# Linear attention and a gated long convolution on one core: two moves in GpSimd's early order, and one add-and-subtract product of batch 6 given to GpSimd

## The chip, the core and the metric

The kernel runs on one core of a Trainium2 chip. A core has a matrix engine (TensorE, PE in the profile), a vector engine (VectorE, DVE), a scalar engine (ScalarE, ACT), a general engine (GpSimd, POOL) and an engine that only issues transfers (SyncE, SP). Each runs its own instructions strictly in program order, and waits on semaphores for the others. Sixteen DMA engines move data between the memory HBM and the on-chip buffer SBUF; transfers are put to them through queues, here mainly SP's and POOL's. TensorE writes its results to eight banks of PSUM, which POOL cannot read.

The metric is the device time of one execution, in microseconds (us). The kernel before took a median of 304.77 us over three runs, from 303.0 to 306.35.

## The reference

There are 8 batches, 8 heads, 576 positions, and 64 channels a head (512 in all). A linear attention is followed by a long convolution with gates:

```
phi(x) = concat(exp(p), exp(-p)),  p = x @ w_phi - max|x @ w_phi|
kv  = phi(k)^T v;   z = sum over positions of phi(k)
att = (phi(q) kv) / (phi(q) z + 1e-6)
x1, x2, x3 = att @ w_proj   (three parts of 512)
y   = x1 * irfft(rfft(x2) * rfft(filter)) * x3
out = y @ w_out
```

The two Fourier transforms over 576 positions are done as matrix products with tables of cosines.

## The kernel before

The program is a list of words, PLAN (lines 31 to 200). Each word names a method, its arguments and often a PSUM bank: `f2,DVE,6,0,0` calls `f2` on VectorE for batch 6, half 0, part 0; `Pk,2,0@6` works in bank 6. `run` (line 1056) goes through the words in order and emits the instructions of each. So the order of the words is the order on each engine's queue, written out by hand, and the engines run apart from one another as far as the data allow. Work of neighbouring batches is interleaved: while batch b is in its convolution, batch b+1 is in its attention.

A batch goes through these stages. Its q, k and v are loaded by POOL's queue (`load`, line 598, 576 KB each, cast to 16 bits on the way). q and k are transposed by a DMA transpose on SP's queue (`trh`, line 627, two of each a batch), only for batch 0 partly by TensorE (`pt`). TensorE makes the projections (`Pk`, `Pq`, `Qn`), DVE the maxima over features (`maxk`, `maxq`, line 732), ACT the exponentials (`ex`, line 718). The maxima of q go through ACT (`mhi`), POOL (`mlo`, line 756, tile mh) and a small TensorE transpose (`trm`, line 760) with its copy (`trme`, tile mT) before `Pq` can subtract them. v is multiplied with the factors of k (`em` by ACT, `vs`, line 774, by POOL or DVE: tiles vp and vm). `KV` (line 789) sums over positions: in each half-head it runs 18 matmuls with vp, then 18 with vm. `NE` (line 803) makes the attention's numerator and denominator, `rc` and `xn` (lines 817, 822) divide.

Then comes the convolution. `f1` (line 871) and `f2` (line 877) are two levels of adds and subtracts (a butterfly) on the attention's output xn, through SD to xf, each on a half of the batch (two of four column blocks); they make the transform shorter. `F` (line 880) is the forward transform: for each block two matmuls with the table Dt (line 883) and four with D on xf (line 887). `X1`, `X2`, `X3` project (lines 944 and 922), `Y1` multiplies with the filter's spectrum (line 932), `m3` adds (line 936), `I` (line 997) transforms back, `ym` gates, `O` (line 1044) is the last product, `st` stores.

The filter's own spectrum is made once, early. Eight pieces of 128 KB are loaded into fl (`fl_load`, line 483) and the middle rows into flt (`fl_loadt`, line 489), all on SP's queue. `fa` (line 498, twice, on POOL) makes sums and differences of the rows, the tile fs; these are the row sums. `zl` (lines 531 to 536, ten small copies on POOL) lays out the lowest frequencies' columns of the cosine tables, the tiles zl2 and zlt. `ft` (on ACT) casts flt to f5 (f in the profile). `Hd` (lines 541 to 551, on TensorE) multiplies: `Hd,4` needs zl2, zlt, fs and f5, and comes first; the others need fs and f5. `He` scales the result into the tables HTe, HTo and H5 that `Y1` reads.

POOL's queue around the first part of the change, in order: `vs,POOL,m,0,0`, `load,k,2`, `vs,POOL,p,0,1`, `w_load,proj,0`, `w_load,proj,1` (the first two of three 512 KB parts of w_proj, line 588), `zl`, `fa,1`, `fa,0`, `f1,POOL,0,0,0`, `load,v,1`, `mlo,1`, `load,q,2`. On SP's queue the transposes `trh,k,2,0` and `trh,k,2,1`, which read what `load,k,2` brings, stand behind `trx,0,1` (line 841, a transpose of xn) and ahead of `trh,q,2,0`.

Around the second part, POOL runs `vs,POOL,p,7,0`, `vs,POOL,m,7,0`, `vs,POOL,p,7,1`; DVE runs `X1e,6,3` and then `f2,DVE,6,0,0` and `tmt,6`. TensorE's order is `F,6,1`, `F,6,0`, `Pq,7,1`, `KV,7,0`. Both blocks of `F` named here belong to half 0, and need the `f2` of that half.

Of the kernel before, what the change touches and what calls it, by code (L numbers as in the profile page):

```python
# [179 lines left out]
KV,7,1@6 m3,POOL,6,0 rc,7,1@4 Y1,6,4@3 xn,7,1@4 Pqt,7@0 KVe,ACT,7,1@6 NE,7,0@2 trx,7,1 exqt,p,7@0  # L180
Pq,7,2@6 rc,7,0@2 exqt,m,7@0 xn,7,0@2 NE,7,3@4 ex,q,p,7,2@6 X2,6,3@0 trx,7,0 f1,POOL,7,0,1
rc,7,3@4 xn,7,3@4 ex,q,m,7,2@6 X2,6,2@3 Y1,6,3@0 f1,POOL,7,0,0 st,SP,5,0,0 X1,6,2@1 st,SP,5,2,0
Y1,6,2@3 f2,POOL,7,0,0 NE,7,2@4 X1e,ACT,6,2@1 X3,6,2@7 m3,DVE,6,1 NEt,7@1 rc,7,2@4 xn,7,2@4
X3,6,3@0 trx,7,2 f1,DVE,7,1,1 I,6,2@4 rct,7@1 f1,POOL,7,1,0 xnt,7,1@1 xnt,7,0@1 X3,6,0@3 Ie,6,2@4
trx,7,3 tm,6,2@7 f2,POOL,7,0,1 Ip,6,2@4 I,6,1@1 Im,6,2@4 trxt,7 tm,6,0@3 I,6,3@6 f2,POOL,7,1,1
Ie,6,1@1 Im,6,1@1 Ie,6,3@6 Ip,6,1@1 X3,6,1@1 f2,POOL,7,1,0 Ip,6,3@6 F,7,1@4 Im,6,3@6 tm,6,1@1
F,7,0@2 ym,POOL,6,2 Fe,ACT,7,1@4 F,7,2@6 Fe,ACT,7,0@2 F,7,3@4 Fe,DVE,7,2@6 ym,POOL,6,1 X1,7,1@1
tm,6,3@0 X1,7,2@7 Fe,DVE,7,3@4 ym,POOL,6,3 I,6,0@2 X2,7,2@5 Ie,6,0@2 X1e,ACT,7,2@7 X2,7,0@4
X1e,ACT,7,1@1 Y1,7,2@5 Xl,ACT,7 X2,7,1@6 Im,6,0@2 X1,7,0@7 Ip,6,0@2 Y1,7,0@4 ym,POOL,6,0 X2,7,3@1
Y1,7,1@6 X1t,7@3 X2,7,4@2 Y1,7,3@1 m3,POOL,7,0 X3,7,2@4 X1te,DVE,7@3 O,6,3@0 Y1,7,4@2 O,6,1@5  # L190
m3,POOL,7,1 Oe,ACT,6,3@0 X1e,ACT,7,0@7 st,SP,6,3,1 X3t,7@0 Oe,ACT,6,1@5 X1,7,3@2 st,SP,5,3,1
tmt,7@0 tm,7,2@4 st,SP,5,3,0 I,7,2@6 st,SP,6,3,0 X3,7,0@5 Ie,7,2@6 st,SP,6,1,0 X1e,ACT,7,3@2
Im,7,2@6 st,SP,6,1,1 I,7,1@0 Ip,7,2@6 tm,7,0@5 ym,POOL,7,2 I,7,0@6 Ie,7,1@0 Ip,7,1@0 I,7,3@4
Ie,7,0@6 Ip,7,0@6 X3,7,1@3 Ie,7,3@4 Im,7,1@0 Im,7,0@6 O,6,0@2 tm,7,1@3 ym,POOL,7,0 X3,7,3@0
Ip,7,3@4 Oe,ACT,6,0@2 Im,7,3@4 ym,POOL,7,1 st,SP,6,0,1 O,6,2@2 tm,7,3@0 st,SP,6,0,0 ym,DVE,7,3
Oe,ACT,6,2@2 O,7,0@1 st,SP,6,2,0 yt,DVE,7 O,7,1@7 Oe,ACT,7,0@1 st,SP,6,2,1 st,ACT,7,0,1 O,7,4@5
st,SP,7,0,0 Oe,ACT,7,1@7 O,7,2@6 st,SP,7,1,1 st,ACT,7,1,0 Oe,DVE,7,4@5 O,7,3@0 st,SP,7,4,1
# [912 lines left out]
```

## Time and profile before

| what | value |
|---|---|
| time, median of three runs | 304.77 us (303.0 to 306.35) |
| the profiled execution's own time | 301.6 us |
| its span in the trace | 299.8 us |
| mean granted clock of TensorE | 0.983 of full speed |
| read from HBM, written | 33.75 MB, 9.44 MB |

The profile is of one execution, and its start times count from the start of the span. A row of a timeline has the start and the duration in us, the engine, the line of the code, the operation, the output and input tiles, how many instructions are merged, and in square brackets the time for which the engine stood idle before it with what ended that idle time. Durations of neighbouring rows on one engine overlap a little, so what a row takes of its engine's time is the distance to the next start. A stretch in the table of busy times gives from:to, its length, and then busy time and count of instructions for PE, PE's weight loads, DVE, ACT and POOL, the granted clock, the share of the DMA engines' time, and GB/s. A row of DMA issues ends with the size and the median time from issue to landing.

### The profile page before, as it was taken

To read this page: it belongs to the slowest core of one execution; us is meant where nothing else is said; L and a number is where in the kernel's file an instruction comes from. 1 tells how busy PE (TensorE), PEld (TensorE's weight loads), DVE (VectorE), ACT (ScalarE), POOL (GpSimd) and SP (SyncE) were. 2 spreads that over 40 slices of the span, in tenths; PEclk is the share of its full clock that TensorE was granted. 3 is DMA by queue.
4 is the path that set the end of the run, shared out by engine and by line. 5 is a ranking of instruction groups with operands and counts; after the bars stand their busy time and mean duration, and the time that the engine had idled before them with its cause. 6 is when DMAs were issued, how large, how long until landed. Compare 5 with 4: busy or idle time off the path is not lost.

```text
span 299.8 us, 10196 instructions
## 1 busy us (share of the span) xinstructions
PE 278.9 (93%) x4303; PEld 198.9 (66%) x4303; DVE 261.8 (87%) x450; ACT 218.2 (73%) x353; POOL 220.5 (74%) x185
## 2 busy tenths in 40 slices
PE   8848679999999999999999999999999898999992
PEld 3525546688677786777776776776687575876761
DVE  8999978899989997889889999899987998897762
ACT  2899988984789777868898498877568978623330
POOL 8008788699888888988979895767686984775640
PEclk9986999999999999999999999999999999999997
DMA  7999999899989979996999626767621641320336
GB/s 112 190 203 181 212 160 198 108 201 180 120 124 190 140 133 183 181 240 124 163 212 198 113 43 148 113 132 135 103 50 29 134 97 37 72 47 0 73 86 195
DMA packets 72734, 40.18 MB, mean 134 GB/s; under 512 B 53040, under 2 KB 67504, under 8 KB 72688
## 3 DMA queue, kind: packets, MB, share of 16 engines
q1 hardware_dynamic: 57472, 22.62, 42.8%
q0 software_dynamic: 14816, 16.25, 34.6%
q8 instruction: 33, 0.54, 0.7%
q10 hardware_dynamic: 400, 0.66, 0.7%
q14 instruction: 13, 0.11, 0.1%
HBM read 33.75 MB, written 9.44 MB: 144 GB/s over the span
## 4 chain that ended last, share of the span: by engine, by line
PE 71%; DVE 10%; DMA 5%; SPq 4%; ACT 3%; issue 2%; POOL 2%; DVEq 0%; ACTq 0%; POOLq 0%
PE ps L944 16%; PE ps L922 11%; PE ps L1044 10%; PE ps L997 7%; PE ps L789 4%; PE ps L803 4%; SPq L627 3%; DMA qn<-in_q_dram 3%; PE ps L883 3%; PE ps L887 3%; DMA flt<-in_moe_filter_fft_dram 2%; PE ps L690 2%; PE ps L953 2%; PE ps L656 2%; PE ps L696 2%
## 5 line engine op out<-in xcount | busy, mean ns | idle before, releaser
L944 PE MATMUL ps<-xT,wproj 128*128 128x256 bf16 x512 | 64.2, 273 | 0.0
L944 PEld LDWEIGHTS <-wproj 128*128 128x128 bf16 x512 | 48.3, 98 | 10.3
L1033 POOL TENSOR_TENSOR yT<-cv,x1s 128x576 bf16<-128x576 f32 x30 | 38.8, 1302 | 16.2 <-DVE cv L1018 13.1
L732 DVE TENSOR_REDUCE mq<-ps 128x8 f32<-128x1024 f32 (+1 forms) x40 | 44.1, 1112 | 3.8 <-PE ps L663 2.4
L732 DVE TENSOR_REDUCE mk<-ps 128x8 f32<-128x1024 f32 (+1 forms) x40 | 44.4, 1113 | 1.0 <-PE ps L671 0.3
L774 POOL TENSOR_TENSOR vp<-vn,vp 128x1152 bf16<-128x1152 bf16 x15 | 33.0, 2201 | 11.0 <-ACT vp L768 10.6
L877 POOL TENSOR_TENSOR xf<-SD 128x512 bf16<-128x512 bf16 x27 | 31.3, 1170 | 8.4 <-PE ps L922 4.4
L936 POOL TENSOR_TENSOR T<-T,T 128x1024 bf16<-128x1024 bf16 x15 | 31.8, 2124 | 6.0 <-DVE T L932 6.0
L1044 PE MATMUL ps<-wout,yT 128*128 128x512 bf16 x144 | 35.6, 379 | 0.2
L718 ACT ACTIVATE Ekm<-ps 128x1024 bf16<-128x1024 f32 x32 | 33.1, 1039 | 2.9 <-PE ps L656 2.3
L718 ACT ACTIVATE Eqm<-ps 128x1024 bf16<-128x1024 f32 x32 | 33.0, 1030 | 2.4 <-PE ps L696 2.2
L718 ACT ACTIVATE Eqp<-ps 128x1024 bf16<-128x1024 f32 x32 | 32.5, 1028 | 2.7 <-PE ps L696 2.5
L718 ACT ACTIVATE Ekp<-ps 128x1024 bf16<-128x1024 f32 x32 | 32.9, 1036 | 1.7 <-DVE mk L732 1.1
L774 POOL TENSOR_TENSOR vm<-vn,vm 128x1152 bf16<-128x1152 bf16 x13 | 28.6, 2204 | 4.3 <-ACT vm L768 4.3
L922 PE MATMUL ps<-wproj,XF 128*128 128x512 bf16 x128 | 31.0, 380 | 0.0
L871 POOL TENSOR_TENSOR SD<-xn 128x512 bf16<-128x512 bf16 x23 | 26.3, 1161 | 5.7 <-DVE xn L822 5.7
L997 PE MATMUL ps<-inv,T 128*128 128x288 bf16 x192 | 27.8, 286 | 0.7 <-DVE xnt L834 0.6
L1018 DVE TENSOR_TENSOR cv<-es,ps 128x288 f32<-128x288 f32 x64 | 25.8, 444 | 1.6 <-ACT es L1015 1.4
L301 ACT COPY o<-ps 128x512 f32<-128x512 f32 x25 | 14.7, 598 | 15.2 <-PE ps L1044 15.1
L1015 ACT COPY es<-ps 128x288 f32<-128x288 f32 x32 | 12.7, 402 | 16.9 <-PE ps L997 15.0
L985 DVE TENSOR_TENSOR x1s<-ps,x1s 128x512 bf16<-128x512 f32 x32 | 21.9, 685 | 2.7 <-PE ps L944 2.2
L822 DVE TENSOR_TENSOR xn<-ps,r 128x512 bf16<-128x512 f32 x32 | 21.8, 687 | 0.9
(175 smaller groups left out, 657.8 us busy)
## 6 DMA issues: line engine op xcount, KB each, us to landing
out_dram<-o SPq DMA_DIRECT2D x67, 128.0 KB, 2.9
vn<-in_v_dram POOLq DMA_DIRECT2D x8, 576.0 KB, 8.0
qn<-in_q_dram POOLq DMA_DIRECT2D x7, 576.0 KB, 8.8
kn<-in_k_dram POOLq DMA_DIRECT2D x7, 576.0 KB, 8.9
wproj<-in_moe_w_proj_dram POOLq DMA_DIRECT2D x3, 512.0 KB, 9.6
fl<-in_moe_filter_fft_dram SPq DMA_DIRECT2D x8, 128.0 KB, 2.9
out_dram<-o ACTq DMA_DIRECT2D x5, 128.0 KB, 3.2
qn<-in_q_dram POOLq DMA_DIRECT2D x2, 288.0 KB, 5.2
```

What stands on the lines that cost most here:

```text
L718: self.nc.scalar.activation(e, p, AF.Exp, bias=0.0, scale=1.0 if g == "p" else -1.0)
L732: self.nc.vector.tensor_reduce(out=out, in_=src, axis=AX.X, op=ALU.max, apply_absolute_value=True)
L774: self.eng(eng).tensor_tensor(out=t[:, :, :, 0:64], in0=self.at("vn", b)[:, 2 * X:2 * X + 2], in1=t[:, :, :, 64:65].to_broadcast([128, 2, ...
L871: self.eng(eng).tensor_tensor(out=o[:, :, 2 * i:2 * i + 2, :], in0=x[:, :, 0:2, :], in1=x[:, :, 2:4, :], op=ALU.subtract if i else ALU.add)
L877: self.eng(eng).tensor_tensor(out=o[:, :, 2 * i:2 * i + 2, :], in0=x[:, :, 0:4:2, :], in1=x[:, :, 1:4:2, :], op=ALU.subtract if i else ALU ...
L922: self.mm(self.pb(0), l, w[:, kt, 512:1024], start=(kt == 0), stop=(kt == 3))
L936: self.eng(eng).tensor_tensor(out=Y, in0=Y, in1=self.at(f"T{2 * e + 1}", b), op=ALU.add)
L944: self.mm(o[:, d], w[:, kt, f0 + 128 * m:f0 + 128 * m + 128], y[:, 1, ::-1, ::-1] if d else y[:, 0], start=(kt == 0), stop=(kt == 3))
L997: self.mm(self.pb(e, 0, 288), l, inv[:, 2 * e + i if i < 2 else 4 + e, :], start=(i == 0), stop=(i == 2))
L1018: self.nc.vector.tensor_tensor(out=self.turn_of("cv", (b, m))[:, :, odd, :], in0=self.turn_of("es", (b, m)).rearrange("p (x t) -> p x t", ...
L1033: self.eng(eng).tensor_tensor(out=self.at("yT", b)[:, m, 0:SEQ], in0=self.turn_of("cv", (b, m)).rearrange("p x h t -> p (x h t)"), in1=sel ...
L1044: self.mm(self.pb(0), y[:, kt, 128 * c:128 * c + 128], w[:, kt, :], start=(kt == 0), stop=(kt == 3))
```

## The change

Three words of PLAN are moved; the total of 1509 words and every method stay.

1. `load,k,2` moves seven places on: on POOL's queue it now stands behind `vs,POOL,p,0,1` and `w_load,proj,0`, ahead of `w_load,proj,1`.
2. `zl,POOL` moves from ahead of `fa,POOL,1` to behind `fa,POOL,0`, just ahead of `f1,POOL,0,0,0`.
3. `f2,DVE,6,0,0` becomes `f2,POOL,6,0,0`, and stands two places later in the list; on POOL's queue that is between `vs,POOL,p,7,0` and `vs,POOL,m,7,0`.

```
-vs,DVE,p,0,0 load,k,2 fl_loadt ex,q,m,0,1@4 Pk,1,1@0 maxq,1,3@2 KV,0,0@6 vs,POOL,p,0,1
-w_load,proj,0 ex,q,p,0,1@4 maxk,1,1@0 KVe,ACT,0,0@6 Pqt,0@4 Qnt,1@2 exqt,p,0@4 NE,0,1@6 maxqt,1@2
-w_load,proj,1 exqt,m,0@4 rc,0,1@6 ex,k,m,1,1@0 NE,0,0@2 xn,0,1@6 zl,POOL fa,POOL,1 Pq,0,3@4
-rc,0,0@2 trx,0,1 ex,k,p,1,1@0 xn,0,0@2 Qn,1,2@6 maxq,1,2@6 ptx,0,0@2 ex,q,p,0,3@4 Qn,1,1@0
-ex,q,m,0,3@4 cols_h ptxe,DVE,0,0@2 maxq,1,1@0 trh,k,2,0 Pq,0,2@2 fa,POOL,0 f1,POOL,0,0,0 ft,ACT
+vs,DVE,p,0,0 fl_loadt ex,q,m,0,1@4 Pk,1,1@0 maxq,1,3@2 KV,0,0@6 vs,POOL,p,0,1 w_load,proj,0
+load,k,2 ex,q,p,0,1@4 maxk,1,1@0 KVe,ACT,0,0@6 Pqt,0@4 Qnt,1@2 exqt,p,0@4 NE,0,1@6 maxqt,1@2
+w_load,proj,1 exqt,m,0@4 rc,0,1@6 ex,k,m,1,1@0 NE,0,0@2 xn,0,1@6 fa,POOL,1 Pq,0,3@4 rc,0,0@2
+trx,0,1 ex,k,p,1,1@0 xn,0,0@2 Qn,1,2@6 maxq,1,2@6 ptx,0,0@2 ex,q,p,0,3@4 Qn,1,1@0 ex,q,m,0,3@4
+cols_h ptxe,DVE,0,0@2 maxq,1,1@0 trh,k,2,0 Pq,0,2@2 fa,POOL,0 zl,POOL f1,POOL,0,0,0 ft,ACT
...
-X1e,ACT,6,0@0 X3t,6@2 Fe,DVE,6,2@6 F,6,3@4 X1e,DVE,6,3@1 O,5,2@0 Fe,ACT,6,3@4 f2,DVE,6,0,0 trm,7@3
-vs,POOL,m,7,0 X1t,6@1 Oe,ACT,5,2@0 F,6,1@4 X1te,ACT,6@1 st,SP,5,2,1 trme,ACT,7@3 F,6,0@6 tmt,6@2
+X1e,ACT,6,0@0 X3t,6@2 Fe,DVE,6,2@6 F,6,3@4 X1e,DVE,6,3@1 O,5,2@0 Fe,ACT,6,3@4 trm,7@3
+f2,POOL,6,0,0 vs,POOL,m,7,0 X1t,6@1 Oe,ACT,5,2@0 F,6,1@4 X1te,ACT,6@1 st,SP,5,2,1 trme,ACT,7@3
...
```

The lines left out at the end hold the same words in the same order, only broken at other places.

More of the change, by code (lines that the diff above doesn't have):

```diff
@@ L174 @@
 st,SP,5,4,0 f2,POOL,6,1,0 X1e,DVE,6,1@7 X1,6,0@0 Oe,ACT,5,3@2 maxk,7,2@3 vs,POOL,p,7,0 F,6,2@6
-X1e,ACT,6,0@0 X3t,6@2 Fe,DVE,6,2@6 F,6,3@4 X1e,DVE,6,3@1 O,5,2@0 Fe,ACT,6,3@4 f2,DVE,6,0,0 trm,7@3
-vs,POOL,m,7,0 X1t,6@1 Oe,ACT,5,2@0 F,6,1@4 X1te,ACT,6@1 st,SP,5,2,1 trme,ACT,7@3 F,6,0@6 tmt,6@2
-Fe,ACT,6,1@4 st,SP,5,0,1 Pq,7,1@0 em,m,7,1 Fe,DVE,6,0@6 KV,7,0@3 ex,q,m,7,1@0 Xl,DVE,6
-vs,DVE,m,7,1 em,p,7,1 Pq,7,0@5 ex,q,p,7,1@0 X2,6,1@7 KVe,DVE,7,0@3 vs,POOL,p,7,1 ex,q,m,7,0@5
-Pq,7,3@1 Y1,6,1@7 ex,q,p,7,0@5 X2,6,0@0 X2,6,4@3 ex,q,p,7,3@1 Y1,6,0@0 NE,7,1@4 ex,q,m,7,3@1
@@ L180 @@
[L180 to L197, printed above, removed]
+X1e,ACT,6,0@0 X3t,6@2 Fe,DVE,6,2@6 F,6,3@4 X1e,DVE,6,3@1 O,5,2@0 Fe,ACT,6,3@4 trm,7@3
@@ new lines @@
+f2,POOL,6,0,0 vs,POOL,m,7,0 X1t,6@1 Oe,ACT,5,2@0 F,6,1@4 X1te,ACT,6@1 st,SP,5,2,1 trme,ACT,7@3
+F,6,0@6 tmt,6@2 Fe,ACT,6,1@4 st,SP,5,0,1 Pq,7,1@0 em,m,7,1 Fe,DVE,6,0@6 KV,7,0@3 ex,q,m,7,1@0
+Xl,DVE,6 vs,DVE,m,7,1 em,p,7,1 Pq,7,0@5 ex,q,p,7,1@0 X2,6,1@7 KVe,DVE,7,0@3 vs,POOL,p,7,1
+ex,q,m,7,0@5 Pq,7,3@1 Y1,6,1@7 ex,q,p,7,0@5 X2,6,0@0 X2,6,4@3 ex,q,p,7,3@1 Y1,6,0@0 NE,7,1@4
+ex,q,m,7,3@1 KV,7,1@6 m3,POOL,6,0 rc,7,1@4 Y1,6,4@3 xn,7,1@4 Pqt,7@0 KVe,ACT,7,1@6 NE,7,0@2
+trx,7,1 exqt,p,7@0 Pq,7,2@6 rc,7,0@2 exqt,m,7@0 xn,7,0@2 NE,7,3@4 ex,q,p,7,2@6 X2,6,3@0 trx,7,0
@@ new lines @@
+f1,POOL,7,0,1 rc,7,3@4 xn,7,3@4 ex,q,m,7,2@6 X2,6,2@3 Y1,6,3@0 f1,POOL,7,0,0 st,SP,5,0,0 X1,6,2@1
+st,SP,5,2,0 Y1,6,2@3 f2,POOL,7,0,0 NE,7,2@4 X1e,ACT,6,2@1 X3,6,2@7 m3,DVE,6,1 NEt,7@1 rc,7,2@4
+xn,7,2@4 X3,6,3@0 trx,7,2 f1,DVE,7,1,1 I,6,2@4 rct,7@1 f1,POOL,7,1,0 xnt,7,1@1 xnt,7,0@1 X3,6,0@3
+Ie,6,2@4 trx,7,3 tm,6,2@7 f2,POOL,7,0,1 Ip,6,2@4 I,6,1@1 Im,6,2@4 trxt,7 tm,6,0@3 I,6,3@6
+f2,POOL,7,1,1 Ie,6,1@1 Im,6,1@1 Ie,6,3@6 Ip,6,1@1 X3,6,1@1 f2,POOL,7,1,0 Ip,6,3@6 F,7,1@4 Im,6,3@6
+tm,6,1@1 F,7,0@2 ym,POOL,6,2 Fe,ACT,7,1@4 F,7,2@6 Fe,ACT,7,0@2 F,7,3@4 Fe,DVE,7,2@6 ym,POOL,6,1
@@ new lines @@
+X1,7,1@1 tm,6,3@0 X1,7,2@7 Fe,DVE,7,3@4 ym,POOL,6,3 I,6,0@2 X2,7,2@5 Ie,6,0@2 X1e,ACT,7,2@7
+X2,7,0@4 X1e,ACT,7,1@1 Y1,7,2@5 Xl,ACT,7 X2,7,1@6 Im,6,0@2 X1,7,0@7 Ip,6,0@2 Y1,7,0@4 ym,POOL,6,0
+X2,7,3@1 Y1,7,1@6 X1t,7@3 X2,7,4@2 Y1,7,3@1 m3,POOL,7,0 X3,7,2@4 X1te,DVE,7@3 O,6,3@0 Y1,7,4@2
+O,6,1@5 m3,POOL,7,1 Oe,ACT,6,3@0 X1e,ACT,7,0@7 st,SP,6,3,1 X3t,7@0 Oe,ACT,6,1@5 X1,7,3@2
+st,SP,5,3,1 tmt,7@0 tm,7,2@4 st,SP,5,3,0 I,7,2@6 st,SP,6,3,0 X3,7,0@5 Ie,7,2@6 st,SP,6,1,0
+X1e,ACT,7,3@2 Im,7,2@6 st,SP,6,1,1 I,7,1@0 Ip,7,2@6 tm,7,0@5 ym,POOL,7,2 I,7,0@6 Ie,7,1@0 Ip,7,1@0
@@ L198 @@
+I,7,3@4 Ie,7,0@6 Ip,7,0@6 X3,7,1@3 Ie,7,3@4 Im,7,1@0 Im,7,0@6 O,6,0@2 tm,7,1@3 ym,POOL,7,0
+X3,7,3@0 Ip,7,3@4 Oe,ACT,6,0@2 Im,7,3@4 ym,POOL,7,1 st,SP,6,0,1 O,6,2@2 tm,7,3@0 st,SP,6,0,0
+ym,DVE,7,3 Oe,ACT,6,2@2 O,7,0@1 st,SP,6,2,0 yt,DVE,7 O,7,1@7 Oe,ACT,7,0@1 st,SP,6,2,1 st,ACT,7,0,1
+O,7,4@5 st,SP,7,0,0 Oe,ACT,7,1@7 O,7,2@6 st,SP,7,1,1 st,ACT,7,1,0 Oe,DVE,7,4@5 O,7,3@0 st,SP,7,4,1
 st,ACT,7,4,0 Oe,DVE,7,2@6 st,SP,7,2,1 st,ACT,7,2,0 Oe,DVE,7,3@0 st,SP,7,3,0 st,ACT,7,3,1
```

## The prediction

> **What bounds the kernel now.** First the page's busy times, its chain that ended last, and the busy times by stretch.
>
> ```profile
> PE 278.9 (93%) x4303; PEld 198.9 (66%) x4303; DVE 261.8 (87%) x450; ACT 218.2 (73%) x353; POOL 220.5 (74%) x185
> ...
> PE 71%; DVE 10%; DMA 5%; SPq 4%; ACT 3%; issue 2%; POOL 2%; DVEq 0%; ACTq 0%; POOLq 0%
> ...
> 50.00:240.00 190.00, 187.73 (x3090) 137.18 (x3087) 170.74 (x269) 150.85 (x243) 158.46 (x117) 1.00 0.85 140
> 246.00:260.00 14.00, 13.02 (x299) 9.13 (x298) 11.60 (x17) 11.44 (x18) 8.16 (x6) 1.00 0.16 35
> ```
>
> PE is busy for 187.73 of the 190 us from 50 to 240 (the third number of a stretch), so an earlier start of that stretch shifts the rest with it. The change works ahead of it, at 26 to 42 us, and behind it at 246, where PE is idle 0.98 of 14 us. In both places I follow the chain of waits: which engine stands, and for whom.
>
> At 26 to 42 us the timelines of POOL, then ACT, then PE, show (start, duration, in brackets the idle time before and its releaser):
>
> ```profile
> 26.49 0.81 POOL L598 DMA_DIRECT2D kn<-in_k_dram  x1
> 27.31 2.46 POOL L774 TENSOR_TENSOR vp<-vn,vp 128x1152 bf16<-128x1152 bf16 x1
> 29.73 1.54 POOL L588 DMA_DIRECT2D wproj<-in_moe_w_proj_dram  x2
> 31.26 0.23 POOL L531 COPY zl<-D 128x32 bf16<-128x32 bf16 x1
> ...
> 32.62 0.23 POOL L536 COPY zlt<-Dt 64x64 bf16<-64x64 bf16 x1
> 34.97 4.66 POOL L498 TENSOR_TENSOR fs<-fl 128x1024 bf16<-128x1024 f32 x2 [2.12 <-DMA fl<-in_moe_filter_fft_dram]
> 39.60 1.15 POOL L871 TENSOR_TENSOR SD<-xn 128x512 bf16<-128x512 bf16 x1
> 40.70 0.78 POOL L598 DMA_DIRECT2D vn<-in_v_dram  x1
> 41.49 0.26 POOL L756 TENSOR_TENSOR mh<-mq,mh 128x36 bf16<-128x36 f32 x1
> ...
> 35.30 0.62 ACT L301 CAST f<-flt 64x512 bf16<-64x512 f32 x1 [0.62 <-DMA flt<-in_moe_filter_fft_dram]
> ...
> 40.48 1.02 ACT L718 ACTIVATE Ekp<-ps 128x1024 bf16<-128x1024 f32 x1
> 42.08 0.27 ACT L301 COPY mT<-ps 128x128 bf16<-128x128 bf16 x1 [0.58 <-PE ps L760]
> ...
> 39.61 0.37 PE L541 MATMUL ps<-f,zlt 64*128 64x512 bf16 x1 [0.64 <-ACT Ekp L718]
> ...
> 41.81 0.23 PE L760 MATMUL ps<-ident,mh 128*128 128x128 bf16 x1 [0.63 <-POOL mh L756]
> ```
>
> The filter's landing holds two engines: POOL stands 2.12 us before the row sums (fs, word fa), ACT 0.62 before the cast of flt (word ft). From there ACT's exponentials run to 41.50 and PE's first filter matmul waits for one of them. POOL's mh (mlo,1) comes late behind the sums, and PE's transpose trm,1 waits 0.63 for it; ACT then 0.58 for trm.
>
> **Step 1: the load of k of batch 2 moves behind vp and the first weights.** The same four instructions stand on POOL from 26.49 to 31.26, in another order: vp 26.49 to 28.91 (27.31 to 29.73 took 2.42), first weights 0.77, k 0.82, second weights 0.77, done at 31.27. Nothing is won in POOL's time; k is issued 3.2 us later (29.7), the first weights 0.8 earlier (28.9). What changes is the traffic beside the filter's loads on SP's queue. SP's issues, then times to landing by issue:
>
> ```profile
> 23.05 2.23 SPq L483 DMA_DIRECT2D fl<-in_moe_filter_fft_dram  x4
> ...
> 26.99 1.05 SPq L483 DMA_DIRECT2D fl<-in_moe_filter_fft_dram  x2
> 28.09 0.49 SPq L489 DMA_DIRECT2D flt<-in_moe_filter_fft_dram  x1
> 31.71 1.23 SPq L841 DMA_TRANSPOSE xT<-xn  x1
> 36.34 6.07 SPq L627 DMA_TRANSPOSE kT<-kn  x2
> ...
> fl<-in_moe_filter_fft_dram SPq DMA_DIRECT2D x2, 128.0 KB, 2.9
> ...
> fl<-in_moe_filter_fft_dram SPq DMA_DIRECT2D x1, 128.0 KB, 5.2
> ...
> fl<-in_moe_filter_fft_dram SPq DMA_DIRECT2D x1, 128.0 KB, 7.1
> flt<-in_moe_filter_fft_dram SPq DMA_DIRECT2D x1, 128.0 KB, 7.2
> ...
> kn<-in_k_dram POOLq DMA_DIRECT2D x1, 576.0 KB, 9.7
> ...
> xT<-xn SPq DMA_TRANSPOSE x1, 10.7
> ```
>
> Issued around 24.4, before k, a piece of 128 KB lands after 2.9 us; issued at 26.99, 27.61 and 28.09, behind k's issue, after 5.2, 7.1 and 7.2. With k away until 29.7, between ends of 2.9 and 7.2, I take 2.9, the row for the same transfer with POOL's queue quiet: the last fl at 27.61 + 2.9 = 30.5, flt at 31.0. The other end is 34.7 and 35.3, as now.
>
> What k's lateness costs: now it lands at 26.49 + 9.7 = 36.2 and SP issues its transposes at 36.34. Behind the first weights I bound it by the 3.2 us later issue: 39.4. SP waits there; behind it stand only transposes for batch 2 (q, from 51 us) and xTt. The first reader of kT comes at 58.55:
>
> ```profile
> 58.55 0.39 PE L656 MATMUL ps<-wphi,kT 64*128 64x128 bf16 x8
> ...
> 45.89 1.92 PE L944 MATMUL ps<-xT,wproj 128*128 128x256 bf16 x16
> ...
> 50.95 2.14 POOL L774 TENSOR_TENSOR vm<-vn,vm 128x1152 bf16<-128x1152 bf16 x1
> ...
> 54.77 0.42 PE L789 MATMUL ps<-vm,Ekm 64*128 64x65 bf16 x16
> ```
>
> The two transposes are issued by 42.4 now and so by 45.6; even 10 us to land leave 3. The xT transpose landed at 42.4 (31.71 + 10.7) for a reader at 45.89; with less queued ahead of it on SP it comes no later. Cost nothing, cover 3 us in each case.
>
> **Step 2: zl moves behind the row sums.** Its ten copies (31.26 to 32.85, 1.59 us) lay inside the wait for the filter. Now fa starts when POOL is free and the filter is there: 31.3. Sums 4.63 (34.97 to 39.60): 35.9. zl 1.59: 37.5. f1 1.10: 38.6. load of v 0.79: 39.4. mh 0.26: 39.7. ACT loses its 0.62 wait, and its exponentials end at 40.88; PE's filter matmul, waiting on ACT, starts at 38.99 and finds zl done. trm,1 came 2.20 after it with 0.63 of waiting, so 1.57 now: 40.56, with mh there. ACT copies mT at about 40.9 in place of 42.08. Steps 1 and 2 together: 1.2 us sooner, and DVE and PE follow from there. If the filter lands at t, mh is ready at t + 8.4: up to 32.1 it costs nothing, at 33.4 the step is even, with t as now trm comes at 43.4, 1.6 late.
>
> **Step 3: one product of batch 6 (f2, half 0) from DVE to POOL.** DVE, POOL, PE in the timelines, and the line's durations (min/median/max):
>
> ```profile
> 246.35 2.08 DVE L877 TENSOR_TENSOR xf<-SD 128x512 bf16<-128x512 bf16 x1
> ...
> 246.00 2.16 POOL L774 TENSOR_TENSOR vm<-vn,vm 128x1152 bf16<-128x1152 bf16 x1
> ...
> 247.10 0.41 PE L883 MATMUL ps<-Dt,xnt 128*128 128x288 bf16 x2
> 248.49 0.42 PE L887 MATMUL ps<-D,xf 128*128 128x144 bf16 x4 [0.98 <-DVE xf L877]
> ...
> 250.08 0.42 PE L789 MATMUL ps<-vm,Ekm 64*128 64x65 bf16 x16
> ...
> L877 POOL TENSOR_TENSOR xf<-SD x27: 1143/1156/1390, 42.5 to 267.2; 128x512 bf16<-128x512 bf16 x27
> ...
> L877 DVE TENSOR_TENSOR xf<-SD x5: 423/426/2083, 44.5 to 246.3; 128x512 bf16<-128x512 bf16 x5
> ```
>
> On DVE it took 2.08 where the others took 0.43, ending 0.28 after POOL's vm did (246.00 + 2.16): it stood behind POOL. It goes to POOL ahead of vm: 246.00 to 247.16. PE's second half of F,6,1 can start 0.24 after the first (247.34, against 248.49): 1.15 won. vm starts at 247.1 and ends at 249.27, while KV's vm matmuls, 1.15 sooner, are due at 248.93: they wait 0.4. Net 0.75; ends 0.5 (a product of 1.39) and 1.15 (vm not late). DVE is freed of 2.08 us and no longer decides. The idle 0.98 us is all that PE has from 246 to 260, so the gain reaches 258.
>
> Here the Trainium skill speaks against the change: GPSIMD Engine Reference, Key points, calls VectorE about 2 times faster for elementwise work. The rows give 0.43 to 1.16 undisturbed; by them alone the move would cost (rival C). The same list names contention of GpSimd with a VectorE instruction of two SBUF inputs; the 2.08 us row beside vm agrees.
>
> **Sum.** 1.2 + 0.75 = 1.95 us off a profiled run of 301.6 gives 299.65. The three runs have their median at 304.77, 3.2 above that one; the forecast is 304.77 - 1.95 = 302.8.
>
> **The rivals.**
> A, slower: the filter lands no sooner, since its own queue (the kT transpose ahead of it) or the first weights delay it. Then zl's 1.59 us lie bare between the sums and mh: trm at 43.4, +1.6, less 0.75: 305.6. It decides from a landing of 33.4 on. For it: the first weights come 0.8 us sooner, 0.9 after flt's issue. Against: pieces issued behind the earlier kT transpose still landed after 2.9.
> B: the 1.2 us are won and lost again, to something that keeps its time. Nearest is v of batch 1: POOL's vm ends at 53.09, KV's vm matmuls would come at 53.57, a margin of 0.5 us. Only step 3 is left: 304.0. Against: v is issued sooner too.
> C: the 2.08 us is an accident of this execution, and DVE's product usually takes 0.43, done by 246.8 ahead of F,6,1. Then step 3 frees no wait and only vm is late: +0.4, with -1.2 before it: 304.0. Against: vm was there for it to stand behind.
>
> **How the numbers follow.** Forecast 0.60, A 0.15, B 0.15, C 0.10. Predicted 302.8. Low end: the median lies 1.8 above the lowest run, and step 3 may bring 0.4 more: 302.8 - 2.2 = 300.6. High end: A with 0.4 of that spread, 306.0. One per cent is 3.05 us, about what a measurement of this kernel can tell from no change. The forecast's 1.95 lies inside; a third of it passes 1% by the spread of 1.8: faster 0.2. A with the spread, and what I have not seen: slower 0.07. Within 0.73.
>
> **What would show it.** Right: fl and flt landing after some 3 us, fa near 31.3, no wait of ACT before ft, trm near 40.6 without waiting for mh; the product on POOL near 1.16 us, F,6,1 without the 0.98 wait, a wait of 0.4 in KV,7,0. Wrong: fa starting after 33.4, PE waiting for zl or mh, kT late at Pk,2,0, KV,1,0 waiting for vm, or new idle PE time after 50 us.

## The result and the profile after

| | before | after |
|---|---|---|
| median of 20 runs each, same chip | 303.59 us (302.01 to 310.9) | 301.40 us (299.83 to 308.04) |
| the profiled execution's own time | 301.6 us | 304.03 us |
| its span | 299.8 us | 302.2 us |

The ratio is 0.9927, 95% interval 0.9901 to 0.9953: the change takes 2.2 us off. Forecast were 1.95 us and 302.8; the 1.4 us between forecast and median lie mostly in the kernel before, whose median over 20 runs is 1.2 below that of the three runs shown. Ratios compare only executions within about 1.5% of their kernel's fastest, medians are over all of them, so the two can differ (in e1, e6 and e8 the median is above that of before and the ratio is not above 1), and the waits in the trace of e6, of an execution outside that bound, bear no argument.

The two profiles stand the wrong way round: the trace of before is one of its kernel's fastest executions, that of after one of its slower ones. Comparing spans would say +2.4 us, where the runs say -2.2. So the place has to be read stage by stage, and from more than one trace. Each trace is cut at five instructions that all have: POOL's first vm (batch 0), PE's first matmul of `X2,0`, PE's `X1t,0`, PE's wait for DVE's cv ahead of `Pk,7,1` (in the stage of batch 6), and DVE's last copy of the output o. All numbers are differences of start times in the timelines.

| trace | first vm at | A: to X2,0 | B: to X1t,0 | C: to the cv wait | D: to the last copy |
|---|---|---|---|---|---|
| before | 23.78 | 27.99 | 9.29 | 172.31 | 61.26 |
| after | 24.97 | 26.76 | 12.00 | 172.64 | 60.52 |
| e5, the change again | 23.77 | 26.84 | 9.55 | 172.30 | 60.52 |
| e9, e12, before again | 23.77, 23.77 | 27.36, 29.95 | 9.29, 9.30 | 172.33, 173.13 | 61.27, 61.27 |

After's start is 1.2 us late before any word of the change is reached, and B is 2.7 longer; A and D are shorter, by 1.2 and 0.74. A and D are what was forecast; B is the part that I had not seen. (Of the fourteen traces below, ten have the first vm at 23.77 to 23.79 and four, after, e1, e4 and e8, at 24.7 to 25.8. No moved word of POOL stands ahead of it; what makes it late is not settled, and no stage counts it.) From the page of after, its chain that ended last, and its busy times by stretch:

```profile
PE ps L944 15%; PE ps L922 9%; PE ps L1044 9%; PE ps L997 6%; DMA kT<-kn 6%; PE ps L789 4%; PE ps L803 4%; PE ps L690 2%; PE ps L663 2%; DVE xn L822 2%; PE ps L696 2%; DVE mk L732 2%; PE ps L953 2%; PE ps L656 2%; PE ps L883 2%
...
50.00:240.00 190.00, 185.45 (x3064) 135.86 (x3062) 168.07 (x265) 148.04 (x237) 155.80 (x115) 1.00 0.88 142
246.00:260.00 14.00, 13.76 (x313) 10.65 (x312) 10.63 (x16) 10.78 (x19) 10.95 (x6) 1.00 0.22 48
```

From 246 to 260 PE is now idle 0.24 us instead of 0.98. From 50 to 240 it is busy for 2.3 us less than before, and the chain that ended last passes with 6% of the span through the transfer of kT, so PE has new idle time there. First the early part of after (POOL, ACT, PE, then SP's issues and the times to landing):

```profile
27.69 3.27 POOL L774 TENSOR_TENSOR vp<-vn,vp 128x1152 bf16<-128x1152 bf16 x1
30.90 0.81 POOL L588 DMA_DIRECT2D wproj<-in_moe_w_proj_dram  x1
31.70 0.76 POOL L598 DMA_DIRECT2D kn<-in_k_dram  x1
32.43 0.77 POOL L588 DMA_DIRECT2D wproj<-in_moe_w_proj_dram  x1
33.19 4.71 POOL L498 TENSOR_TENSOR fs<-fl 128x1024 bf16<-128x1024 f32 x2
...
40.47 0.79 POOL L598 DMA_DIRECT2D vn<-in_v_dram  x1
...
35.97 0.62 ACT L301 CAST f<-flt 64x512 bf16<-64x512 f32 x1
...
41.75 0.23 PE L760 MATMUL ps<-ident,mh 128*128 128x128 bf16 x1
...
27.01 1.09 SPq L483 DMA_DIRECT2D fl<-in_moe_filter_fft_dram  x2
28.14 0.49 SPq L489 DMA_DIRECT2D flt<-in_moe_filter_fft_dram  x1
41.53 8.46 SPq L627 DMA_TRANSPOSE kT<-kn  x2
...
fl<-in_moe_filter_fft_dram SPq DMA_DIRECT2D x2, 128.0 KB, 2.9
flt<-in_moe_filter_fft_dram SPq DMA_DIRECT2D x1, 128.0 KB, 2.7
kT<-kn SPq DMA_TRANSPOSE x2, 12.6
```

The filter's last pieces land after 2.9 and 2.7 us; POOL and ACT no longer stand for them (no brackets at 33.19 and 35.97). In spite of a start 1.2 late, trm comes at 41.75, where it came at 41.81. Then PE stands twice for kT of batch 2:

```profile
54.15 0.40 PE L656 MATMUL ps<-wphi,kT 64*128 64x128 bf16 x8 [0.84 <-DMA kT<-kn]
...
61.15 0.23 PE L671 MATMUL ps<-wphi,kT 64*128 64x128 bf16 x2 [1.51 <-DMA kT<-kn]
```

And the late part, POOL and PE:

```profile
249.01 1.15 POOL L877 TENSOR_TENSOR xf<-SD 128x512 bf16<-128x512 bf16 x1
250.12 2.15 POOL L774 TENSOR_TENSOR vm<-vn,vm 128x1152 bf16<-128x1152 bf16 x1
...
250.10 0.41 PE L883 MATMUL ps<-Dt,xnt 128*128 128x288 bf16 x2
250.34 0.41 PE L887 MATMUL ps<-D,xf 128*128 128x144 bf16 x4
...
252.33 0.43 PE L789 MATMUL ps<-vm,Ekm 64*128 64x65 bf16 x16 [0.24 <-POOL vm L774]
```

The product takes 1.15 us on POOL, `F,6,1` goes on without a wait, and the vm matmuls of `KV,7,0` have a wait of 0.24.

### The profile page after: what moved, and what is told of

It is laid out like the page before. It is cut to its first block, busy times and chain, and to the rows that moved or that the text cites. A ratio compares the mean times of both kernels' runs of the same rounds, so it can differ in the third digit from the quotient of the medians.

```text
span 302.2 us, 10196 instructions
## 1 busy us (share of the span) xinstructions
PE 280.2 (93%) x4303; PEld 200.2 (66%) x4303; DVE 260.0 (86%) x449; ACT 218.4 (72%) x353; POOL 222.6 (74%) x186
## 3 DMA queue, kind: packets, MB, share of 16 engines
q1 hardware_dynamic: 57472, 22.62, 43.1%
## 4 chain that ended last, share of the span: by engine, by line
PE 66%; DVE 15%; DMA 7%; POOL 4%; issue 4%; ACT 3%; DVEq 0%; ACTq 0%; POOLq 0%
PE ps L944 15%; PE ps L922 9%; PE ps L1044 9%; PE ps L997 6%; DMA kT<-kn 6%; PE ps L789 4%; PE ps L803 4%; PE ps L690 2%; PE ps L663 2%; DVE xn L822 2%; PE ps L696 2%; DVE mk L732 2%; PE ps L953 2%; PE ps L656 2%; PE ps L883 2%
## 5 line engine op out<-in xcount | busy, mean ns | idle before, releaser
L774 POOL TENSOR_TENSOR vp<-vn,vp 128x1152 bf16<-128x1152 bf16 x15 | 33.8, 2254 | 8.8 <-ACT vp L768 8.0
L877 POOL TENSOR_TENSOR xf<-SD 128x512 bf16<-128x512 bf16 x28 | 32.4, 1171 | 8.4 <-PE ps L922 4.4
L1015 ACT COPY es<-ps 128x288 f32<-128x288 f32 x32 | 12.8, 403 | 16.9 <-PE ps L997 15.0
L932 DVE TENSOR_TENSOR T<-ps,HTo 128x1024 bf16<-128x1024 f32 x16 | 19.3, 1218 | 4.5 <-PE ps L922 3.1
```

Of the source, the lines that this page charges most:

```text
L774: self.eng(eng).tensor_tensor(out=t[:, :, :, 0:64], in0=self.at("vn", b)[:, 2 * X:2 * X + 2], in1=t[:, :, :, 64:65].to_broadcast([128, 2, ...
L877: self.eng(eng).tensor_tensor(out=o[:, :, 2 * i:2 * i + 2, :], in0=x[:, :, 0:4:2, :], in1=x[:, :, 1:4:2, :], op=ALU.subtract if i else ALU ...
```

## The experiments

The theory: (1) k's load slowed the filter's loads, and moving it frees the row sums; (2) zl behind the sums lets them start sooner; (3) the product on VectorE was slow beside POOL's vm. Rivals: the filter is no sooner (A), the early gain is lost again (B), the slow product is an accident (C); and, once kT's waits were seen, that k's lateness costs what the filter gains. The first four kernels take the change apart.

### e1: step 1 alone

```
-... load,k,2 fl_loadt ... vs,POOL,p,0,1 w_load,proj,0 ...
+... fl_loadt ... vs,POOL,p,0,1 w_load,proj,0 load,k,2 ...
```

> Step 1 alone: the load of k of batch 2 behind vp and the first weights; zl stays ahead of the row sums and the product of batch 6 stays on VectorE. Theory: the filter lands about 2.9 us after its issue (2.7 to 3.0 in the profile after), and since POOL's row sums and zl together are the same 6.2 us in either order, this step alone brings all of the early gain: 1.2 to 1.5 us faster than before, ratio 0.995 to 0.996, ACT without its 0.6 us wait before the cast of flt and PE's trm without its wait for mh. In the profile, zl runs ahead of the sums, and sums and zl end where they do with the change. Rival K: the late k takes it back: PE waits for kT at its first reader (0.84 and 1.51 us in the profile after), and the ratio is 1.000 or above. Rival S: the early gain is nothing and all of the 2.2 us measured comes from the product of batch 6: ratio 1.000.

Measured: ratio 0.995 (0.9903 to 0.9997), that is -1.5 us; the median over all twelve executions, 305.80, is above that of before beside them, 303.30, so the time alone is weak evidence and the trace has to carry it. A is 26.59, B 11.44. The filter's pieces land after 2.8 (fl) and 4.6 us (flt). PE's waits beyond half a microsecond in B and in batch 6 (line numbers of e1 to e4 are 3 lower than elsewhere):

```profile
60.18 0.23 PE L668 MATMUL ps<-wphi,kT 64*128 64x128 bf16 x2 [1.87 <-DMA kT<-kn]
...
251.11 0.42 PE L884 MATMUL ps<-D,xf 128*128 128x144 bf16 x4 [0.99 <-DVE xf L874]
```

So the load alone wins the early part, brings the wait for kT with it, and leaves the 0.99 in batch 6, which belongs to step 3.

### e2: step 2 alone

```
-... zl,POOL fa,POOL,1 ... fa,POOL,0 f1,POOL,0,0,0 ...
+... fa,POOL,1 ... fa,POOL,0 zl,POOL f1,POOL,0,0,0 ...
```

> Step 2 alone: zl behind the row sums, everything else as before. Theory: with k's load where it was the filter still lands 5 to 7 us after its issue, the row sums start at about 35 us, and zl's 1.59 us lie bare behind them: PE's first filter matmul waits about 1.6 us longer (for zl), mh comes 1.6 us later, and the kernel is 1.6 us slower than before, ratio about 1.005. Rival: the order of zl and the sums is of no account since the wait is taken up behind it: ratio 1.000.

Measured: 0.8% slower, 1.0076 (1.0035 to 1.0117). A is 32.62, 4.6 longer than in before. The sums start 1.7 later, since this execution's filter is later still; the other 2.9 lie behind them, with zl's 1.59 and a granted clock of 0.80 from 33 to 50 us (1.00 in before). With k in its old place the filter is late, and zl, no longer under that wait, lies bare behind the sums (POOL, then PE):

```profile
36.64 4.65 POOL L495 TENSOR_TENSOR fs<-fl 128x1024 bf16<-128x1024 f32 x2 [5.38 <-DMA fl<-in_moe_filter_fft_dram]
...
43.09 0.60 PE L538 MATMUL ps<-f,zlt 64*128 64x512 bf16 x1 [2.27 <-POOL zlt L533]
```

This is the cost that rival A would have had. Step 2 is only harmless together with step 1.

### e3: step 3 alone

```
-... f2,DVE,6,0,0 trm,7@3 vs,POOL,m,7,0 ...
+... trm,7@3 f2,POOL,6,0,0 vs,POOL,m,7,0 ...
```

> Step 3 alone: one product of batch 6 on POOL ahead of vm, the early part as before. Theory: PE's wait of about 1 us in F of batch 6 is gone, a wait of 0.2 to 0.4 us for vm in KV of batch 7 appears, net 0.75 us: ratio 0.9975. Rival S: this is the whole of the change's gain, 2.2 us: ratio 0.993. Rival C: the 2.08 us product on VectorE was an accident of one execution and the move only makes vm late: 0.4 us slower, ratio 1.001.

Measured: 1.0036 (0.9995 to 1.0076), which by itself says nothing: the code of its early part is that of before, and varies by more than the effect. D says it: 60.50, and in its trace stands the same small wait as in after:

```profile
254.33 0.43 PE L786 MATMUL ps<-vm,Ekm 64*128 64x65 bf16 x16 [0.23 <-POOL vm L771]
...
39.03 0.62 ACT L298 CAST f<-flt 64x512 bf16<-64x512 f32 x1 [3.74 <-DMA flt<-in_moe_filter_fft_dram]
```

The second row is from its early part: flt landed 9.9 us after its issue, against 7.2 in the profile of before, with the same words in the same order up to there. A is 32.57. Some 1 us of it is not the filter: `X2,0` starts 17.9 us behind the start of the sums, against 16.8 in before, and the granted clock from 33 to 50 us was 0.70, against 1.00. Still, the profile of before was not the worst case.

### e4: steps 1 and 2

```
-... load,k,2 fl_loadt ... w_load,proj,0 ... zl,POOL fa,POOL,1 ... fa,POOL,0 f1,POOL,0,0,0
+... fl_loadt ... w_load,proj,0 load,k,2 ... fa,POOL,1 ... fa,POOL,0 zl,POOL f1,POOL,0,0,0
```

> Steps 1 and 2 together, the product of batch 6 left on VectorE. Theory: the same as step 1 alone within 0.3 us (the filter is there when POOL comes free, so the order of zl and the sums changes nothing): 1.2 to 1.5 us faster than before, ratio 0.995 to 0.996. If step 2 has a worth of its own, this one is faster than step 1 alone by up to 1.6 us. Rival K: PE waits for kT and the ratio is 1.000 or above.

Measured: 0.9972 (0.994 to 1.0004). A is 26.95, against 26.59 in e1 with zl in front: no gain from step 2. B is 9.91, D 61.25.

### e5: the change again

> The change itself, once more, as the partner of the three runs beside it. Measured so far inside the traces: from POOL's first vm to PE's first X2 matmul 26.6 to 27.0 us wherever k's load is moved (three executions), against 28.0 and 32.6 where it is not; from that matmul to X1t of batch 0 9.9 to 12.0 us against 9.3, the surplus being waits for kT; from the last cv wait of batch 6 to the last copy 60.5 us with the product on POOL (two executions), 61.25 with it on VectorE (four). Theory: the same again: 26.6 to 27.0, a surplus of 0.6 to 2.7, 60.5; ratio 0.993 as measured. Rival: the lateness of kT in the profile after was an accident of one execution: surplus 0 and PE not waiting for kT.

Measured: 0.993 (0.9887 to 0.9973), like the first time. Its trace starts where that of before does (first vm at 23.77 and 23.78), which makes it the best pair. POOL, then PE:

```profile
26.50 3.26 POOL L774 TENSOR_TENSOR vp<-vn,vp 128x1152 bf16<-128x1152 bf16 x1
...
31.99 4.69 POOL L498 TENSOR_TENSOR fs<-fl 128x1024 bf16<-128x1024 f32 x2
...
40.65 0.23 PE L760 MATMUL ps<-ident,mh 128*128 128x128 bf16 x1 [0.22 <-POOL mh L756]
```

The sums start at 31.99 (34.97 before), trm comes at 40.65 (41.81 before), A is 1.15 shorter, B 0.26 longer, D 0.74 shorter: 1.63 us in all, 1.65 by the two last copies (294.63 and 292.98). PE does not stand for kT here.

### e6: k ahead of both weights

Against the change:

```
-... vs,POOL,p,0,1 w_load,proj,0 load,k,2 ... w_load,proj,1 ...
+... vs,POOL,p,0,1 load,k,2 w_load,proj,0 ... w_load,proj,1 ...
```

> The change, but k's load behind vp and ahead of both weight loads: 0.8 us sooner, with 512 KB less in front of it on POOL's queue. Theory: the filter (issued by 28.1, k at about 30) still lands 3 us after its issue, so the early part stays at 26.6 to 27.0 us, and k lands 3 us or so sooner, so that PE's waits for kT (0.6 to 2.7 us) mostly go: up to 2 us faster than the change. Rival: what delays kT is not k's own landing but SP's transposes being slow beside the loads of v and q that follow; then kT comes as late as with the change and the time is the same. Rival: k alongside the filter again holds it back, and the early part is 28 us or more.

Measured: 0.9964 (0.9925 to 1.0003), medians 305.10 and, for before, 304.41; bringing k sooner shows no gain over the change. In its trace PE stands 1.95 and 1.64 us for the products of v in `KV,1,0`; e8 and e10 test whether v is late elsewhere too.

### e7: k behind both weights

Against the change:

```
-... w_load,proj,0 load,k,2 ... w_load,proj,1 ...
+... w_load,proj,0 ... w_load,proj,1 load,k,2 ...
```

> The change, but k's load behind both weight loads: 0.8 us later, with 512 KB more in front of it. It makes the suspected cost larger. Theory: the early part stays at 26.6 to 27.0 us, kT comes 2 to 3 us later, PE waits for it at Pk,2,0 (0.84 us in the profile after) for 2 to 3.5 us, and the kernel is 1 to 3 us slower than the change, ratio to before about 1.000. Rival: kT is set by SP's transposes or by PE's own pace and the time is that of the change.

Measured: 0.9875 (0.984 to 0.991), 300.43 us: the fastest kernel here. A is 26.75, B 9.29, and PE never stands for kT, although k lands as late as anywhere (at 43.1). The expectation, 1 to 3 us slower than the change, was wrong. POOL, PE and SP, and then how long the transposes took to land:

```profile
32.12 4.67 POOL L498 TENSOR_TENSOR fs<-fl 128x1024 bf16<-128x1024 f32 x2
39.41 0.79 POOL L598 DMA_DIRECT2D vn<-in_v_dram  x1
...
40.57 0.23 PE L760 MATMUL ps<-ident,mh 128*128 128x128 bf16 x1 [0.23 <-POOL mh L756]
...
43.26 6.16 SPq L627 DMA_TRANSPOSE kT<-kn  x2
...
kT<-kn SPq DMA_TRANSPOSE x2, 7.9
```

Issued 1.7 us after those of the change's profile, the transposes land after 7.9 us instead of 12.6. So the lateness of k is not what PE paid for in after and e1; it was that the transposes themselves were slow. The intervals of e7 and e6 do not overlap; those of e7 and the change do.

### e8: k in its old place, the filter ahead

The three last filter loads are put ahead of a transpose on SP's queue, and k goes back ahead of vp; steps 2 and 3 are in. Against the kernel before, for the loads:

```
-... trh,k,1,1 ... fl_load,1,0 ... fl_load,2,1 ... load,k,2 fl_loadt ...
+... fl_load,1,0 fl_load,2,1 fl_loadt trh,k,1,1 ... load,k,2 ...
```

> The other way to the same end: k's load stays where it was before (ahead of vp), and the last three filter loads (two fl, one flt) go ahead of the second kT transpose of batch 1 on SP's queue, 1.6 us sooner; zl and the product of batch 6 as in the change. Theory: it is the filter's landing that counts, not k's place; issued by 26.5 the three pieces land by about 30, the early part is again 26.6 to 27.0 us, k lands at about 36 as before and PE never waits for kT of batch 2: 1 to 2.5 us faster than the change, ratio to before 0.985 to 0.99. Rival: the traffic beside k now slows the kT transpose of batch 1, which stands behind the filter, from 3.6 to 7 us or more; PE's Pk,1,3 waits for it and the early part is 28 us or longer.

Measured: 1.0 (0.9954 to 1.0047), medians 307.50 and, for before, 304.41. The filter lands after 2.9 to 3.0 us and A is 26.83, as good as with k moved; so what matters for the filter is that it is ahead of k. In this trace that is in part its late start: with the first vm at 25.82, k was issued at 28.53, 1.5 us behind the last filter piece (27.04); in an execution that starts as before does (k at 26.49) that piece would still be behind k. And v of batch 1 now lands after 11.5 us, and PE stands for POOL's product of it in `KV,1,0`:

```profile
vn<-in_v_dram POOLq DMA_DIRECT2D x1, 576.0 KB, 11.5
...
56.54 0.43 PE L789 MATMUL ps<-vm,Ekm 64*128 64x65 bf16 x16 [0.73 <-POOL vm L774]
```

### e9 and e12: the kernel before, run twice more

> The kernel before, looked at again. Theory (the profile of before that the prediction was read from was a lucky execution): the last filter pieces land 7 to 10 us after their issue, and from POOL's first vm to PE's first X2 matmul it is 28.0 us or more, up to 32.6, as in e2 and e3. Rival (the 28.0 of that profile is the rule and e2 and e3 were the exceptions): 27.5 to 28.5 us, landing after 7.2 at most.

> The kernel before a third time. Theory: again 28.0 us or more from POOL's first vm to PE's first X2 matmul, most of it from the filter's landing after 7 to 10 us. Rival: 27.5 to 28.5 us as in the profile of before.

Measured: A is 27.36 in e9 and 29.95 in e12. e9 lies below both expectations, nearer the rival's, with flt landing after 6.6; e12 lies in the theory's. So the 28.0 of the profile of before is one of a spread, towards its lower end, and no lucky exception. POOL's wait for the filter, in e9 and then in e12:

```profile
34.31 4.67 POOL L498 TENSOR_TENSOR fs<-fl 128x1024 bf16<-128x1024 f32 x2 [1.46 <-DMA fl<-in_moe_filter_fft_dram]
```

```profile
36.81 4.65 POOL L498 TENSOR_TENSOR fs<-fl 128x1024 bf16<-128x1024 f32 x2 [3.97 <-DMA fl<-in_moe_filter_fft_dram]
```

Over the traces with k issued ahead of the last filter pieces the wait is 1.46 to 5.63 us long, and PE's start of `X2,0` follows it: in before, e9 and e12 it comes 16.8 to 16.9 us behind the start of the sums. SP may have a part in it: the pieces are issued behind a kT transpose, at 27.02 in e9 and 27.89 in e12. No run varies that alone.

### e10: k ahead of the weights, v of batch 1 ahead of the sums

Against e6:

```
-... load,k,2 w_load,proj,0 ... w_load,proj,1 ... fa,POOL,1 ... load,v,1 ... mlo,POOL,1
+... load,k,2 w_load,proj,0 ... w_load,proj,1 ... load,v,1 fa,POOL,1 ... mlo,POOL,1
```

> The load of k ahead of both weights, as in e6, and the load of v of batch 1 moved ahead of the row sums, so that it is on its way before kT's transposes are issued. Theory (in e6 v was late because kT's transposes, issued at 36, ran beside v and the weights): v, issued near 32, lands before 45, the waits of PE in KV,1,0 (1.95 and 1.64 us) are gone, X2first to X1t is 9.3 to 10 us, ratio 0.986 to 0.993. Rival (what is held back is simply whatever comes last on POOL's queue): v lands, but q of batch 2 or kT itself is late by as much, PE waits 1.5 to 3.5 us there, ratio 0.996 to 1.0.

Measured: 0.9944 (0.9923 to 0.9964), at neither expectation. The theory failed: v, issued 8 us sooner, landed only at 48.5. And kT's transposes, beside it, were the slowest of all:

```profile
31.98 0.78 POOL L598 DMA_DIRECT2D vn<-in_v_dram  x1
35.59 12.76 SPq L627 DMA_TRANSPOSE kT<-kn  x2
58.92 0.23 PE L671 MATMUL ps<-wphi,kT 64*128 64x128 bf16 x2 [0.45 <-DMA kT<-kn]
...
vn<-in_v_dram POOLq DMA_DIRECT2D x1, 576.0 KB, 16.5
...
kT<-kn SPq DMA_TRANSPOSE x2, 18.2
```

PE paid only 0.45 for kT and nothing for v. Its A is 27.80, some 1 us above the others with k moved. Two things in its trace are late by nearly as much. The row sums start at 32.73, 0.7 behind those of e5, since the issue of v (0.78) stands ahead of them. And PE's transposes of xn start at 33.42, 0.8 behind those of e5, with a granted clock of 0.69 from 24 to 34 us against 0.85. The second is not the move's: they are late in e3 and e12 too (33.28 and 33.31), whose early words are those of before. Which of the two A follows is not separated.

### e11: k behind both weights, zl ahead of the sums

Against e7:

```
-... w_load,proj,1 load,k,2 ... fa,POOL,1 ... fa,POOL,0 zl,POOL ...
+... w_load,proj,1 load,k,2 ... zl,POOL fa,POOL,1 ... fa,POOL,0 ...
```

> The load of k behind both weights and the product on POOL, as in e7, but zl left ahead of the row sums. Theory (step 2 has no worth of its own once the filter lands early): within 0.3% of e7, ratio 0.984 to 0.991, no wait of PE for zlt. Rival 1 (the prediction's step 2: ACT's copy of flt and POOL's mh come 0.6 to 1.2 us later with zl in front): 0.988 to 0.995. Rival 2 (zl belongs in front, since it fills a wait): 0.980 to 0.984.

Measured: 0.9892 (0.9866 to 0.9918), 300.7 us; within 0.2% of e7, A 26.71 and B 9.29. The sums start 1.4 us later than in e7 (33.55, against 32.12), ACT does not stand for flt, and trm comes at 40.42, against 40.57:

```profile
33.55 4.66 POOL L498 TENSOR_TENSOR fs<-fl 128x1024 bf16<-128x1024 f32 x2
...
34.25 0.63 ACT L301 CAST f<-flt 64x512 bf16<-64x512 f32 x1
...
40.42 0.23 PE L760 MATMUL ps<-ident,mh 128*128 128x128 bf16 x1 [0.28 <-POOL mh L756]
```

So moving zl is worth nothing: the ten copies take POOL's time on either side of the sums, and mh stands behind all of them.

## Why the prediction was right, and where it was not

**Step 1, the filter.** Right. With k moved, flt lands after 2.7 to 4.6 us (forecast 2.9); with k ahead of it, after 6.6 to 9.9 in the traces that show it. A is 26.6 to 27.0 in e1, e4, e5, e7, e11 and after (and 27.80 in e10, for the reasons given there), against 27.4 to 32.6 in before, e3, e9 and e12. In after, e1 and e4 POOL's first vm, and so k, was 0.9 to 2.1 us late while SP issued the filter at the usual time, which by itself gave the filter a lead; e5, e7 and e11, which start as before does, have 26.7 to 26.8 and carry the comparison. Rival A is refuted. The Trainium skill, page "DMA: Bandwidth & Descriptors", section "Issuing engines are not separate DMA queues", says that transfers started by different engines run on the same 16 DMA engines and interleave; the filter on SP's queue behind k on POOL's agrees.

**Step 1, POOL's time.** Off by 0.7. I had the row sums start at 31.3; in e5 POOL is free at 31.99. I took vp at 2.42 from the row of before, but, begun at 26.50 directly behind vm, it took 3.26. VectorE runs its own product of that kind beside it, in before and in e5:

```profile
26.32 1.45 DVE L774 TENSOR_TENSOR vp<-vn,vp 128x1152 bf16<-128x1152 bf16 x1
...
26.31 1.44 DVE L774 TENSOR_TENSOR vp<-vn,vp 128x1152 bf16<-128x1152 bf16 x1
```

POOL's vp ends at 29.77 in before and at 29.76 in e5, and in all fourteen traces 2.0 us after VectorE's ends. Begun sooner, it ended no sooner: the 0.8 us for the issue of k, which had cost nothing ahead of vp, now come behind it. The prediction met the same in step 3, where VectorE's product stood behind POOL's, and did not look for it here. The result hardly changed: trm at 40.65, forecast 40.56.

**Step 1, k's lateness.** Here a step failed. "Cost nothing, cover 3 us in each case" rested on 58.55 as the first reader of kT. That is `Pk,2,1`; `Pk,2,0` stands 5.4 us ahead of it, with the same line and tiles, in the trace of before:

```profile
53.18 0.39 PE L656 MATMUL ps<-wphi,kT 64*128 64x128 bf16 x8
```

For that reader the prediction's own bound (issued by 45.6, 10 us to land) is 2.4 us late. And "even 10 us to land" was too little: the transposes took 12.4 to 13.9 us in after, e1 and e5. PE paid 2.35 us in after and 1.87 in e1, and nothing in e5. B, at 9.29 or 9.30 in before, e2, e3, e9 and e12, is 12.00, 11.44, 9.91 and 9.55 in after, e1, e4 and e5: 1.4 us longer on average. In after and e1 nearly all of it is kT. In e4 and e5 about 0.3 us is another transpose, xTt, issued behind those of kT on SP's queue: it took 8.8 and 8.2 us to land, against 4.0 in before, and `X1t,0` starts as it lands. The prediction put nothing on it. In e4:

```profile
62.69 0.64 PE L950 MATMUL ps<-xTt,wproj 128*128 128x64 bf16 x16 [0.17 <-DMA xTt<-xnt]
```

**Why the sum still came out.** What I missed on either side is of one size. The mean of A in the four traces with the early code of before (before, e3, e9, e12) is 29.5, that of after, e1, e4 and e5 is 26.8: a gain of 2.7, less B's 1.4, leaves 1.3, where the forecast had 1.2; with step 3's 0.74 that is 2.0 of the 2.2 measured. It is an estimate from four traces each, and without the 1 us that e3 has beside its lower clock it would be 1.0 in place of 1.3. That the two cancel is luck. The forecast was read off an execution with one of the shorter waits, and left out a loss; in the pair before and e5, which has neither extreme, the change wins 1.65.

**Step 2.** Its reasoning was right in each row and empty as a step: e1 against e4 (A 26.59 and 26.95) and e11 against e7 (0.9892 and 0.9875) show no gain from it, and e2 shows what it costs where the filter is late. The 1.2 us belong to the load alone.

**Step 3.** Right in mechanism and size. In six traces with the product on VectorE (before, e1, e2, e4, e9, e12) D is 61.25 to 61.27 and the product takes 2.08 to 2.10; in eight with it on POOL D is 60.50 to 60.53. The forecast was 0.75 net, with vm 0.4 late (249.27 less 248.93, its own rows, is 0.34); measured are 0.74 and an idle time of 0.24. Rival C, and with it the rule of the Trainium skill that had VectorE faster for elementwise work (GPSIMD Engine Reference, Key points), does not decide here: beside POOL's vm the VectorE product took 2.08 to 2.10 every time.

**Rival B** named v of batch 1; in after POOL stood 0.70 for it and PE not at all. The early gain was eaten in part, but by kT. Whether a run gets e5's or after's share of that is not settled.

## What to carry to other kernels

Before a load is called covered, list every reader of its tile by name, not by the row that looks like it, and price a transfer by what it takes beside the traffic it will meet, not by its own row of before. Where a wait is for a transfer, take several traces of the kernel before: here that wait ran from 1.5 to 5.6 us, more than the whole effect. And a load that is needed later can be worth putting last: behind both weights k cost PE nothing, and that kernel (e7) is 1.25% faster than before, with an interval of 0.9 to 1.6%. That it beats the change itself is not shown, since their intervals overlap.

## What the hardware showed that I had not expected

The DMA engines can be busy all the time and move little. From 50 to 56 us both after and e7 have transposes on SP's queue (q1: what is left of kT, then q and xn) while POOL's queue (q0) loads. Packets, bytes and share of the 16 engines' time; after first, e7 second:

```profile
DMA packets 1647, 0.59 MB, mean 98 GB/s; under 512 B 1433, under 2 KB 1647, under 8 KB 1647
...
q1 hardware_dynamic: 1416, 0.35, 99.3%
q0 software_dynamic: 231, 0.23, 47.2%
```

```profile
DMA packets 3337, 1.24 MB, mean 206 GB/s; under 512 B 2824, under 2 KB 3336, under 8 KB 3336
...
q1 hardware_dynamic: 2808, 0.69, 84.8%
q0 software_dynamic: 528, 0.52, 68.0%
```

Sixteen engines for 6 us are 96 engine-microseconds; a packet of q1 took 0.993 x 96 / 1416 = 67 ns in after and 29 ns in e7 (0.848 x 96 / 2808), for packets of the same mean size (0.25 KB). The shares add up to more than 100%, so packets of the two queues overlap in time. Both queues are busy in both cases, so the mere presence of the other queue does not explain it; what sets off the slow stretch stays open. Nor does the distance between v's load on POOL's queue and kT's transposes on SP's give a rule: issued 1.1 us behind v the transposes took 12.6 us to land (after), 3.6 behind 18.2 (e10), 3.9 behind 7.9 (e7), and ahead of v 8.6 in the trace of before. No kernel here varied that distance alone.
